# Four strips of 32 columns for each 64-row product, and P V in two bursts

## The chip, the cores and the metric

The kernel runs on one core of one Trainium2 chip. The metric is the time of one execution on the device, in microseconds (us). Times of this kernel are medians of a few executions; the profile is that of one execution, taken by the hardware profiler, and it has a time of its own.

The engines are named as the profile names them: PE (TensorE, matrix products), PEld (its weight loads, which overlap with the products), DVE (VectorE), ACT (ScalarE), POOL (GpSimd) and SP (SyncE, which here only issues DMAs and wake-ups). L709 is line 709 of the kernel.

## What is computed

A layer with two branches over a sequence of 2,048 tokens of 448 features. One branch is local attention with 16 heads of 28 features, in which each token sees itself and seven earlier ones, two apart; the other is a two-layer MLP with 1,792 hidden features. The branches are multiplied and added to the input.

```python
def _A_ref(x, wqkv, wo):                       # H = 16, Dh = 28, W, dil = 8, 2
    qkv = (x @ wqkv).reshape(B, S, 3, H, Dh).transpose(2, 0, 3, 1, 4)
    q, k, v = qkv[0], qkv[1], qkv[2]
    idx = pos[:, None] - (jnp.arange(W) * dil)[None, :]
    mask = idx >= 0
    ...
    logits = jnp.einsum("bhsd,bhswd->bhsw", q, kg) * Dh ** -0.5
    logits = jnp.where(mask[None, None, :, :], logits, -1e9)
    o = jnp.einsum("bhsw,bhswd->bhsd", _softmax(logits), vg)
    return o.transpose(0, 2, 1, 3).reshape(B, S, D) @ wo

def _B_ref(x, w1, b1, w2, b2):
    return gelu(x @ w1 + b1) @ w2 + b2

xn = _layernorm(A_x)
return A_x + _A_ref(xn, A_wqkv, A_wo) * _silu(_B_ref(xn, B_w1, B_b1, B_w2, B_b2))
```

Data and weights are bf16.

## The kernel before

**Tokens.** Even and odd tokens never see each other (the dilation is 2), so the sequence is split into two halves, and then into 16 tiles of 128 tokens and four chunks of 512. For the attention it is cut again into nine blocks (`VIS`), each with four windows of 57 (or 56) queries against 64 keys.

**The order is planned.** Nothing is issued where it is written. Each piece of work is a task with an engine (or several to choose from), an assumed cost in us, tasks it depends on, a priority, buffers it takes and gives back, and a function that issues the instructions. `_Plan.run` plays the tasks on a model of the engines: at each step it finds the task that could start first, looks at all that could start on that engine within 0.12 us of it, and picks the one with the highest priority. `emit` then issues all tasks in that order, so every engine runs a fixed program. The priorities are the tables `PRIO` and `LATER`. On PE, a task has a mode, the tiling shape in which PE's array is used. A task in another mode than the last is charged `SWITCH` = 0.095 us, one in the same mode gets `SAME` = 20 added to its priority.

**Dense products.** 448 features are three tiles of 128 rows and one of 64. The projections to q, k and v (L532 and L556) and the first MLP layer (L591) are computed as seven half products of 64 rows per output, not as three and a half whole ones. `pair` (L477) takes two outputs: four steps with the top rows of one beside the bottom rows of the other, then, after a wake-up sent through POOL or SP once the first four are done, three steps the other way round. In a step, two products of 64 rows by 128 columns run side by side, each into its own PSUM bank. The very first projections are made with 128 rows (`first_batch`). The second MLP layer (L627) and the output projection (L796) are 128-row products.

**Attention.** For each block, `scores_of` issues 64 products of 32 rows by 64 columns (L677) into four banks. ACT takes the exponential (L687), a 0/1 mask is multiplied in on DVE or POOL (L693), and `values_of` issues 64 products of 64 rows by 32 columns (L709), P V, into two banks. DVE then divides by the sums (L719 to L733). The keys' v rows are first moved to their places by DMAs that POOL issues (L354).

A PE task of the attention is a visit, made by `attn` (L743) from the list `VISITS` (L24): the scores of the first two blocks alone, and then P V of each block with the scores of the block two further on, in one task. A task with P V has mode 33, one with scores mode 32. It takes two banks for P V and four for scores, together, of eight.

**End.** `final_part` (L792) makes the output projection, multiplies, adds the input (DVE, or POOL for the first eight tiles) and writes out by SP.

Of the kernel before, what the change touches and what calls it, by code (L numbers as in the profile page):

```python
# [17 lines left out]
TILED = 30  # L18
SAME = 20
HOPS = ("POOL", ("SP", "POOL"))  # L20
MASK_ON = (("DVE", "POOL"), (0.4, 1.2))


def VISITS(bs):  # L24
    out = [[("S", b)] for b in bs[:2]]
    for i, b in enumerate(bs):
        out.append([("P", b)] + [("S", c) for c in bs[i + 2:i + 3]])
    return out
# [11 lines left out]
class _Task:  # L40
    __slots__ = ("eng", "cost", "deps", "fn", "prio", "take", "give", "slots",
                 "start", "end", "on", "ndep", "users", "tail", "seq", "table", "limit", "mode", "out")


class _Plan:
# [7 lines left out]
    def add(self, eng, cost, fn, deps=(), prio=0, take=(), give=(), tail=0.0, table=(), limit=None,  # L53
            mode=128):
# [5 lines left out]
        t.mode, t.out = mode, None  # L60
# [14 lines left out]
    def _at(self, t, e, free):  # L75
        at = free.get(e, 0.0)
        for p, n in t.take.items():
            if len(p.free) < n or p.fifo and p.fifo[0] is not t:
                return None
            at = max(at, sorted(p.free)[n - 1][0] + HOP)  # L80
        if t.table and self.table not in t.table:
            at += TABLE
        for d in t.deps:
            at = max(at, d.end - d.tail if d.on == e else d.end + HOP)
        if e == "PE" and t.mode != self.mode:
            at = max(at, free.get(e, 0.0) + SWITCH)
        return at

    def run(self):
# [6 lines left out]
        self.mode = 128  # L96
        ready = [t for t in self.tasks if not t.ndep]
        order = []
        while ready:
# [14 lines left out]
            tiled = first[2] == "PE" and self.mode < 64  # L114
            at, t, e, c = min(near, key=lambda k: (-k[1].prio - (TILED if tiled and k[1].mode < 64 else SAME if k[2] == "PE" and k[1].mode == self.mode else 0),
# [4 lines left out]
            if e == "PE" and t.fn is not None:  # L120
                self.mode = t.out or t.mode
# [43 lines left out]
def kernel(  # L165
# [80 lines left out]
    def ring(name, n, shape, dt=BF16, fifo=False):  # L246
# [24 lines left out]
        "project": (49.5, 205, 104, 52.5,),  # L271
        "project2": (147, 150, 101, 61,),
        "values": (89.5, 62.5, 21, 58,),
        "attn": (185, 179.5, 78, 174.5, 106.5, 106, 138.5, 136.5, 32.5,),
        "ff1": (185, 180, 84.5, 176.5, 66.5, 64.5, 156.5, 189.5, 203, 146, 76, 114.5, 77.5, 179.5,
            75.5, 118.5, 180.5, 14.5, 163, 68, 151, 115.5, 194.5, 167.5, 180, 188.5, 86, 93,),
        "gelu": (62.5, 22.5, 95, 92.5,),
        "ff2": (144, 162.5, 103.5, 142.5, 44.5, 112.5, 67, 5, 89, 106.5, 101.5, 75, 74, 55, 11.5,
            6.5,),
        "final": (140, 19.5, 70.5, 47, 112, 34.5, 23.5, 142.5, 73, 53, 198.5, 188.5, 81.5, 126.5,  # L280
            180, 71,),
        "norm": (37.5, 132, 179.5, 129.5, 74.5, 99, 161, 69, 63, 62, 43.5, 73, -5.5, 90, 133.5,
            150,),
        "loads": (166.5, 166, 188, 139.5, 54.5,),
        "stats": (47.5, -60, 180.5, 23, 127, 56, 188.5, 77, 197.5, -13.5, 185, 205.5, 138, 14, 52.5,
            138.5,),
        "turn_x": (108.5, -1, 28, 116, 210, 116.5, 131.5, 160, 41.5, 79.5, 70, 119, -4.5, 74.5,
            132.5, 111,),
        "turn_qk": (68.5, 112, 174.5, 90, 80, 6, 149.5, 60.5, 4, 140.5, 199.5, 96.5, 103, 166.5,
            140, 156,),  # L290
        "move_v": (81.5, 95, 23, 95, 18.5, 26.5, 8, 128, 29.5,),
        "copies": (50, 119.5, 58.5, 76, 32.5, 135.5, 43, 1, 87, 79.5, 129, 77, 32, 41.5, 135,),
    }
    LATER = {"swap": 135, "qk": 165, "v": 29.5, "gelu": 30.5, "exp": 55.5, "mask": -60, "pv": 45, "recip": -16.5, "os": 54.5, "y": 153.5, "tanh": 182.5, "g": 58, "sg": 183, "o": 120.5}
# [174 lines left out]

    def together(top, bottom):  # L470
        return [(f(), g()) for f, g in zip(top, bottom, strict=True)]
# [5 lines left out]
    def pair(a, b, prio, early=False):  # L477
# [11 lines left out]
        def f2(k):  # L489
            held["told"] = (nc.gpsimd if k.on == "POOL" else nc.sync).nop()  # L490
            for i in held["last"]:
                behind(held["told"], i)
        told = plan.add(HOPS[0] if early else HOPS[1], 0.06, f2, [t], 300)

        def f3(k):
            p, q = buf(p_b, t, 0), buf(p_b, t, 1)
            for i in together([part(b, q, kt, 0, kt + 4) for kt in range(3)], [part(a, p, kt, 1, kt + 4) for kt in range(3)])[0]:
                behind(i, held["told"])
# [5 lines left out]
    def first_batch(tiles, prio, tiles0=0):  # L504

        f = []
        for kt in range(3):
            for i, js in enumerate(tiles):
                def f1(k, kt=kt, i=i, js=js):
                    for q, j in enumerate(js):  # L510
                        j.part(buf(p_b, f[i] if kt else k, q), kt, 2, kt == 0, False)
# [14 lines left out]
    def qk_rows(t, which, prio):  # L526
        cs = slice(t * P, (t + 1) * P)

        def part(ps, kt, half, start, stop):
            r = half_rows(half)  # L530
            w = w_in[r, kt, which * D:(which + 1) * D] if kt < 3 else w_in3[r, 0, :]
            return nc.tensor.matmul(ps[:, :D], xnT[r, kt, cs], w, start=start, stop=stop)  # L532

        def evac(a, own, i):
# [6 lines left out]
            if len(t_row[t]) == 2:  # L541
                t_qk[t] = dma_T(qkT[:, :, :, cs].rearrange("p w g c -> p (w g) c"), lambda: b[:].rearrange("p w h c -> p (w h c)"),
                                t_row[t], PRIO["turn_qk"][t], None, 2, 1.9 if t < 3 else 3.8 if t == TPC else 2.0 if t == TPC + 1 else 1.27)
# [6 lines left out]
    def vproj(t, prio):  # L550
        k0 = t * P

        def part(ps, kt, half, start, stop):
            r = half_rows(half)
            w = w_in[r, kt, 2 * D:] if kt < 3 else w_in3[r, 1, :]
            return nc.tensor.matmul(ps[:, :D], xnT[r, kt, k0:k0 + P], w, start=start, stop=stop)  # L556
# [7 lines left out]
    def values(b):  # L564

        t_v[b], v_at[b] = [], []
        for i in range(2):
            first = None
            for w in range(2):
                k0 = VIS[b][2][w][i][1]  # L570
                for lo in sorted({k0, max(k0, (k0 + NK - 1) // P * P)}):
# [6 lines left out]
                    t_v[b].append(d)  # L578
# [6 lines left out]
    def ff1(c, mt, prio, gate):  # L585
# [3 lines left out]
        def part(ps, kt, half, start, stop):  # L589
            r = half_rows(half)  # L590
            return nc.tensor.matmul(ps[:], w1[r, kt, ms], xnT[r, kt, cs], start=start, stop=stop)  # L591
# [74 lines left out]
    def scores_of(b):  # L666
        q, nq, wins = VIS[b]

        def fn(banks):
            for i in range(2):  # L670
                for g in range(G):
                    for hl in range(4):
                        for w in range(2):
                            r = slice(32 * hl, 32 * hl + 32)
                            q0, k0 = wins[w][i]
                            c0 = (G * i + g) * nq
                            nc.tensor.matmul(banks[hl][NK * w:NK * w + NK, c0:c0 + nq], qkT[r, 1, g, k0:k0 + NK],  # L677
                                             qkT[r, 0, g, q0:q0 + nq], start=True, stop=True)
        return fn, [t_qk[t] for t in range(wins[0][0][1] // P, (q + 4 * nq - 1) // P + 1)]

    def weights_of(b, a, at, prio, gate):
# [3 lines left out]
        for hl in range(4):  # L685
            def f2(k, hl=hl):
                nc.scalar.activation(buf(p_E, k)[:, :n], buf(p_b, a, at + hl)[:, :n], ACT.Exp, scale=SCALE)  # L687
            e = plan.add("ACT", act(n), f2, [a] + gate, prio + LATER["exp"], take=(p_E,), give=((p_b, a, at + hl),), table=("exp",))
# [8 lines left out]
    def values_of(b, exps):  # L697
        nq = VIS[b][1]

        def fn(banks):  # L700
            for hl in range(4):
                E = buf(p_E, exps[hl])
                for i in range(2):
                    v = buf(*v_at[b][i])
                    for g in range(G):
                        for w in range(2):
                            r = slice(NK * w, NK * w + NK)
                            c0, c1 = (2 * hl + i) * nq, (G * i + g) * nq
                            nc.tensor.matmul(banks[w][32 * g:32 * g + 32, c0:c0 + nq], v[r, 4 * g + hl, :],  # L709
                                             E[r, c1:c1 + nq], start=True, stop=True)  # L710
        return fn, tuple((p_E, e, 0) for e in exps) + tuple(v_at[b])

    def output_of(b, po, i, w, prio):
# [4 lines left out]
        def f5(k):  # L718
            nc.vector.transpose(buf(p_dt, k)[:, :32 * m], buf(p_b, po, i)[:, :32 * m])  # L719
        d = plan.add("DVE", dve(32 * m), f5, [po], prio + LATER["recip"], take=(p_dt,))  # L720
# [11 lines left out]
        def f8(_):  # L732
            nc.vector.tensor_tensor(out=oT[:, :, q0:q0 + 2 * nq],  # L733
                                    in0=buf(p_b, po, i)[:, :n].rearrange("p (l q) -> p l q", l=4),
                                    in1=buf(p_dt, d)[:, :n].rearrange("p (l q) -> p l q", l=4), op=ALU.mult)
        o = plan.add("DVE", dve(n), f8, [rb], prio + LATER["os"], give=((p_b, po, i), (p_dt, d, 0)))
# [3 lines left out]
    last_visit = {"S": [], "P": []}  # L740
    state = {}

    def attn(b, what):  # L743

        deps, take, give, fns, cost = [], [], (), [], -SWITCH
        for n, (w, blk) in enumerate(what):
            if not n or what[n - 1][0] != w:
                cost += SWITCH
            cost += 0.215
            if not n:  # L750
                cost += 0.03
            at = len(take)
            if w == "S":
                fn, d = scores_of(blk)
                d = d + state["early"]
                take += [p_b] * 4
                fns.append(lambda k, fn=fn, at=at: fn([buf(p_b, k, at + i) for i in range(4)]))
            else:
                exps, masked = state[blk]
                fn, g = values_of(blk, exps)  # L760
                give += g
                d = masked + t_v[blk]
                take += [p_b] * 2
                fns.append(lambda k, fn=fn, at=at: fn([buf(p_b, k, at + i) for i in range(2)]))
            deps = deps + d + last_visit[w][-1:]

        def f1(k):
            for fn in fns:
                fn(k)
        prio = PRIO["attn"][b]  # L770
        a = plan.add("PE", cost, f1, deps, prio + (LATER["pv"] if what[0][0] == "P" else 0), take=take, give=give, tail=0.15,
# [195 lines left out]
```

## Time and profile before

| what | us |
|---|---|
| median of 3 executions (158.08 to 158.12) | 158.12 |
| the profiled execution | 157.98 |
| its span, from first to last instruction | 156.2 |
| PE busy in that span | 150.1 |
| lines 591 and 627 in the chain that ended last | 23% and 22% |
| lines 532, 556 and 796 in it | 11%, 6% and 7% |
| lines 677 and 709 (scores and P V) in it | 4% and 4% |

The chain that ended last is followed back from the last instruction, at each step to what released it, or to the instruction before it on its engine. Lengths of products on PE are modelled and overlap, so neighbouring lengths may add up to more than the time between their starts. A line `x64` in a timeline is 64 instructions merged into one row.

Of the 36 mask products (L693), 28 ran on POOL and 8 on DVE. The page's row of instruction packets (queue q8) gives number, MB and share of 16 engines' span: these bring the instructions of PE from memory.

### The profile page before, as it was taken

Reading aid. Unit: us, or ns where it says so; the run is one execution under the profiler, and the core shown is the slowest. Engines: PE = TensorE matmul, PEld = TensorE weight load, DVE = VectorE, ACT = ScalarE, POOL = GpSimd, SP = SyncE. Lnnn points to the kernel's source line nnn. Section 1 sums busy time; section 2 is a strip of 40 time slices with the busy share of each in tenths; the row PEclk is TensorE's granted clock in tenths of the full one; section 3 lists DMA queues with packets and bytes.
Section 4 is the critical chain, followed back from the end, with each engine's and each line's share of the span. In section 5 each row is a group of like instructions: output and inputs, shape, how many; then the busy total and the mean of one; then the engine's idle time right before and its main releaser. Section 6 shows DMA issues by size and latency. Waiting matters only on the chain.

```text
span 156.2 us, 5305 instructions
## 1 busy us (share of the span) xinstructions
PE 150.1 (96%) x2204; PEld 77.8 (50%) x2204; DVE 113.2 (72%) x259; ACT 83.3 (53%) x149; POOL 74.7 (48%) x123
## 2 busy tenths in 40 slices
PE   6999999999999999999999999999999999999980
PEld 2544454444455555455554644455556444545570
DVE  4789551486266758997799895109899996998992
ACT  3245867378889416444634149782496587051220
POOL 7854856000459408839261098389599780000000
PEclk9999999999999999999999999999999999999999
DMA  4999969999749443099039822123300100200211
GB/s 156 329 317 315 167 124 187 237 269 307 141 95 166 64 82 90 10 192 138 4 83 85 131 70 73 38 76 83 105 0 4 34 31 29 63 4 0 68 36 43
DMA packets 33575, 17.36 MB, mean 111 GB/s; under 512 B 25331, under 2 KB 32387, under 8 KB 33552
## 3 DMA queue, kind: packets, MB, share of 16 engines
q1 hardware_dynamic: 31472, 14.03, 41.3%
q0 software_dynamic: 1936, 2.88, 8.5%
q8 instruction: 17, 0.28, 0.8%
q10 hardware_dynamic: 144, 0.11, 0.2%
q14 instruction: 6, 0.05, 0.1%
HBM read 7.06 MB, written 1.84 MB: 57 GB/s over the span
## 4 chain that ended last, share of the span: by engine, by line
PE 80%; DVE 8%; DMA 3%; POOL 2%; issue 2%; ACT 1%; SPq 1%; DVEq 0%; ACTq 0%; POOLq 0%
PE bank L627 23%; PE bank L591 22%; PE bank L532 11%; PE bank L796 7%; PE bank L556 6%; PE bank L677 4%; PE bank L709 4%; PE bank L327 3%; DMA xnT<-xn 3%; POOL v L354 2%; DVE sg L801 2%; DVE o L807 1%; DVE w_in L659 1%; ACT E L687 1%; DVE xn L438 1%
## 5 line engine op out<-in xcount | busy, mean ns | idle before, releaser
L627 PE MATMUL bank<-w,h 128*128 128x448 bf16 (+1 forms) x238 | 45.2, 342 | 0.0
L591 PE MATMUL bank<-xnT,w 64*128 64x512 bf16 x392 | 44.7, 376 | 0.0
L595 ACT ACTIVATE h<-bank,b 128x512 bf16<-128x512 f32 x56 | 34.0, 689 | 12.9 <-PE bank L591 12.8
L354 POOL DMA_DIRECT2D v<-v_tok x52 | 27.6, 538 | 19.8 <-PE bank L709 9.0
L693 POOL TENSOR_TENSOR E<-E,m_gen 128x456 bf16<-128x456 bf16 x24 | 26.7, 1139 | 11.7 <-ACT E L687 9.5
L627 PEld LDWEIGHTS <-h 128*128 128x128 bf16 x238 | 22.3, 98 | 18.1 <-issue 0.4
L591 PEld LDWEIGHTS <-w 64*128 64x128 bf16 x392 | 19.1, 94 | 22.7 <-issue 1.1
L532 PE MATMUL bank<-w_in,xnT 64*128 64x448 bf16 (+1 forms) x212 | 24.3, 350 | 0.1
L687 ACT ACTIVATE E<-bank 128x456 bf16<-128x456 f32 (+1 forms) x36 | 17.0, 555 | 9.1 <-PE bank L677 9.1
L655 ACT ACTIVATE t<-y 128x448 f32<-128x448 f32 x15 | 8.7, 578 | 17.4 <-DVE y L649 17.4
L719 DVE STREAM_TRANSPOSE dt<-bank 128x480 f32<-128x480 f32 (+1 forms) x18 | 12.1, 671 | 5.6 <-PE bank L709 5.6
L532 PEld LDWEIGHTS <-xnT 64*128 64x128 bf16 (+1 forms) x212 | 10.6, 94 | 10.9 <-issue 1.1
L314 DVE CAST qk_tok<-bank 128x448 bf16<-128x448 f32 x16 | 9.4, 613 | 6.8 <-PE bank L532 6.8
L796 PE MATMUL bank<-wo,oT 128*128 128x448 bf16 (+1 forms) x68 | 14.1, 342 | 0.0
L312 ACT CAST qk_tok<-bank 128x448 bf16<-128x448 f32 x16 | 8.3, 533 | 10.6 <-PE bank L532 10.0
L556 PE MATMUL bank<-w_in,xnT 64*128 64x448 bf16 (+1 forms) x106 | 13.4, 349 | 0.0
L649 DVE TENSOR_TENSOR y<-bank,b 128x448 f32<-128x448 f32 x15 | 9.3, 620 | 4.9 <-PE bank L627 4.9
L728 DVE STREAM_TRANSPOSE dt<-rd 128x480 f32<-128x480 f32 (+1 forms) x18 | 12.1, 673 | 0.5
L733 DVE TENSOR_TENSOR oT<-bank,dt 128x456 bf16<-128x456 f32 (+1 forms) x18 | 11.3, 630 | 0.5
L404 DVE BATCH_NORM_STATS2 st<-x_sb 128x6 f32<-128x448 bf16 x16 | 9.6, 603 | 2.4 <-DMA x_sb<-in_A_x_dram 2.4
L438 DVE TENSOR_SCALAR xn<-x_sb,mv,rstd 128x448 bf16<-128x448 bf16 x16 | 6.3, 394 | 6.0 <-POOL rstd L426 5.8
L796 PEld LDWEIGHTS <-oT 128*128 128x128 bf16 x68 | 6.3, 98 | 6.3 <-issue 0.8
(62 smaller groups left out, 128.9 us busy)
## 6 DMA issues: line engine op xcount, KB each, us to landing
out_dram<-o SPq DMA_DIRECT2D x15, 112.0 KB, 1.7
w<-in_B_w_dram SPq DMA_DIRECT2D x2, 784.0 KB, 7.2
w<-in_B_w_dram SPq DMA_DIRECT2D x2, 672.0 KB, 7.0
x_sb<-in_A_x_dram SPq DMA_DIRECT2D x3, 448.0 KB, 6.3
v<-v_tok POOLq DMA_DIRECT2D x20, 64.0 KB, 2.5
w_in<-in_A_wqkv_dram SPq DMA_DIRECT2D x3, 336.0 KB, 4.3
w<-in_B_w_dram SPq DMA_DIRECT2D x4, 112.0 KB, 6.5
wo<-in_A_wo_dram POOLq DMA_DIRECT2D x4, 98.0 KB, 4.2
```

Of the source, the lines that this page charges most:

```text
L354: nc.gpsimd.dma_start(dst(k), src())
L532: return nc.tensor.matmul(ps[:, :D], xnT[r, kt, cs], w, start=start, stop=stop)
L556: return nc.tensor.matmul(ps[:, :D], xnT[r, kt, k0:k0 + P], w, start=start, stop=stop)
L591: return nc.tensor.matmul(ps[:], w1[r, kt, ms], xnT[r, kt, cs], start=start, stop=stop)
L595: nc.scalar.activation(buf(p_h, own, i)[:], buf(p_b, own, i)[:], ACT.Gelu_apprx_tanh, bias=b1[:, mt:mt + 1])
L627: nc.tensor.matmul(ps[:, :n], buf(*h_at[(c, mt)])[:, j * P:(j + 1) * P], w2[:, mt, cs], start=(mt == 0 and not biased), stop=(mt == NMT - 1))
L687: nc.scalar.activation(buf(p_E, k)[:, :n], buf(p_b, a, at + hl)[:, :n], ACT.Exp, scale=SCALE)
L693: (nc.gpsimd if k.on == "POOL" else nc.vector).tensor_tensor(out=E[:, :n], in0=E[:, :n], in1=m[:, :n], op=ALU.mult)
L719: nc.vector.transpose(buf(p_dt, k)[:, :32 * m], buf(p_b, po, i)[:, :32 * m])
L728: nc.vector.transpose(buf(p_dt, d)[:, :32 * m].rearrange("p (b c) -> p b c", c=32), buf(p_rd, r)[:, :m].unsqueeze(2).to_broadcast((P, m, 32)))
L733: nc.vector.tensor_tensor(out=oT[:, :, q0:q0 + 2 * nq], in0=buf(p_b, po, i)[:, :n].rearrange("p (l q) -> p l q", l=4), in1=buf(p_dt, d)[:, ...
L796: nc.tensor.matmul(ps[:, :n], oT[:, kt, t * P:(t + 1) * P], wo[:, kt, cs], start=(kt == 0), stop=(kt == KT - 1))
```

## The change

1. Each product of 64 rows and 128 columns is issued as four with 32 columns, into the four quarters of the bank's partitions, with the same moving operand (`strips`). `together` interleaves them: first strip of the one output, first strip of the other, second strip, and so on. Whole products of 128 rows stay as they are.
2. P V is issued in two tasks of 32 products, one for each `i` (half of the windows). They are in mode 64, the same as the dense half products. The first gives back one of the two v tiles, the second the other and the E tiles. It waits for all four masked E tiles and its own v tile only.
3. Scores are a task of their own with 64 products, in mode 32. Scores and P V bursts are marked `thin`; a thin task right after another is charged `APART` = 0.25 us. `VISITS` is gone: in each stage all scores are added, then all P V.
4. The masks are on DVE alone.
5. b2 is loaded as one row and spread over the partitions by POOL, where a DMA spread it.
6. All priorities are new, and some assumed costs of the transposing DMAs.

```diff
-TILED = 30
+APART = 0.25
-MASK_ON = (("DVE", "POOL"), (0.4, 1.2))
+MASK_ON = ("DVE", 0.4)
...
+        if e == "PE" and t.thin and self.thin:
+            at = max(at, free.get(e, 0.0) + APART)
...
+    def strips(out, lhsT, rhs, half, start, stop):
+        n = P if half > 1 else 32
+        return [lambda c=c: nc.tensor.matmul(out[c:c + n], lhsT[:, c:c + n], rhs, start=start, stop=stop) for c in range(0, P, n)]
+
     def together(top, bottom):
-        return [(f(), g()) for f, g in zip(top, bottom, strict=True)]
+        done = []
+        for f, g in zip(top, bottom, strict=True):
+            done.append([q() for pair in zip(f(), g(), strict=True) for q in pair])
+        return done
...
-            for i in held["last"]:
-                behind(held["told"], i)
+            behind(held["told"], held["last"][-1])
...
-            return nc.tensor.matmul(ps[:], w1[r, kt, ms], xnT[r, kt, cs], start=start, stop=stop)
+            return strips(ps[:], w1[r, kt, ms], xnT[r, kt, cs], half, start, stop)
...
-        def fn(banks):
+        def fn(banks, i):
+            v = buf(*v_at[b][i])
             for hl in range(4):
                 E = buf(p_E, exps[hl])
-                for i in range(2):
-                    v = buf(*v_at[b][i])
-                    for g in range(G):
-                        for w in range(2):
...
+                for g in range(G):
+                    for w in range(2):
...
+    def visit(what, fn, deps, prio, n, give):
+        parts = []
+        whole = what == "S"
+        for i in range(1 if whole else 2):
+            def f1(k, i=i):
+                own = (parts or [k])[0]
+                for q in range(2) if whole else (i,):
+                    fn([buf(p_b, own, j) for j in range(n)], q)
+            parts.append(plan.add("PE", 0.5 if whole else 0.15, f1, deps[i] + deps[1] * whole + [(parts or [last_visit[what]])[-1]], prio + i * LATER["half"],
+                                  take=() if i else (p_b,) * n, give=give[i] + give[1] * whole, tail=0.15, mode=32 if whole else 64, thin=True))
+        last_visit[what] = parts[-1]
+        return parts[0], parts[-1]
...
-    t_b2 = dma("POOL", b2[:], B_b2.rearrange("(o d) -> o d", o=1).to_broadcast((P, D)), 112, 82, turned)
+    b2r = p_o.bufs[-1]
+    t_b2r = dma("POOL", b2r[:1], B_b2.rearrange("(o d) -> o d", o=1), 1, 82, turned[:1])
+    t_b2 = plan.add("POOL", 0.5, lambda _: nc.gpsimd.partition_broadcast(b2[:], b2r[:1], channels=P), [t_b2r], 82)
```

## The prediction

> **What bounds the kernel.** I read the page first: busy shares, slices, chain of waits.
>
> ```profile
> span 156.2 us, 5305 instructions
> PE 150.1 (96%) x2204; PEld 77.8 (50%) x2204; DVE 113.2 (72%) x259; ACT 83.3 (53%) x149; POOL 74.7 (48%) x123
> PE   6999999999999999999999999999999999999980
> PEclk9999999999999999999999999999999999999999
> PE 80%; DVE 8%; DMA 3%; POOL 2%; issue 2%; ACT 1%; SPq 1%; DVEq 0%; ACTq 0%; POOLq 0%
> q8 instruction: 17, 0.28, 0.8%
> ```
>
> TensorE (PE) is busy in every slice but the ends, at full clock, and has 80% of the chain. So the time is the sum of what PE issues, plus some 4.5 us after its last product (151.7 to 156.2). A change counts by what it takes off PE's row; anything on another engine counts only where PE comes to wait for it.
>
> Next the timeline of PE alone (start, length, line, shape, count). Lengths overlap, so I use distances between starts.
>
> ```profile
> 57.62 0.68 PE L709 MATMUL bank<-E,v 64*32 64x57 bf16 x64
> 58.23 0.76 PE L677 MATMUL bank<-qkT 32*64 32x57 bf16 x64
> 58.92 2.82 PE L627 MATMUL bank<-w,h 128*128 128x448 bf16 x14
> ...
> 76.80 2.82 PE L532 MATMUL bank<-w_in,xnT 64*128 64x448 bf16 x28
> 79.46 2.81 PE L556 MATMUL bank<-w_in,xnT 64*128 64x448 bf16 x28
> 82.11 2.81 PE L532 MATMUL bank<-w_in,xnT 64*128 64x448 bf16 x28
> 84.85 1.69 PE L796 MATMUL bank<-wo,oT 128*128 128x448 bf16 x8
> ```
>
> Read three prices. A step of two 64-row products side by side: (79.46-76.80)/14 = 0.190 us at 448 columns; the group from 13.24 to 16.27 gives 3.03/14 = 0.216 us at 512. A change of tiling shape: 84.85-82.11 = 2.74 against 14 x 0.190 = 2.66, so about 0.09 us, paid by whoever comes next. P V: 58.23-57.62 = 0.61 us for 64 tiny products.
>
> Then stretches of that P V visit, each counted from its start, in the windows of line 709 (length; PE busy, products started so far; clock; DMA):
>
> ```profile
> 57.62:57.74 0.12, 0.12 (x32) 1.00 0.18 22
> 57.62:57.84 0.22, 0.22 (x32) 1.00 0.11 12
> 57.62:58.11 0.49, 0.49 (x64) 1.00 0.05 5
> ```
>
> This is the centre of the case. The first 32 products start within 0.12 us (3.7 ns each); then nothing starts for 0.10 us; the other 32 need 0.27 us (8.3 ns each), and the drain into the next shape fills the 0.61. So 32 products lie ready when a visit begins, and whatever is beyond must be fed at 8.3 ns.
>
> **Part 1, P V in two bursts of 32.** Before: five visits alone at 0.61 (3.05), two double visits of 1.29 and 1.25 us, together 5.59; seven entries from another shape at 0.09 make 6.2 us. After, 18 bursts. One between strips of its own shape costs 0.12 us, no drain on either side, and the stretch without starts lies under the next dense step of 0.19. One put among 128-row products costs 0.09 + 0.12 + about 0.12 (the step from a visit's last product to the next shape: 0.61-0.49) = 0.33. Ends: all in 64-row stretches, 18 x 0.12 = 2.2; none, 5.9. The planner charges 0.095 for a switch and adds 20 to the rank of work in the standing mode, so I take two thirds inside: 12 x 0.12 + 6 x 0.33 = 3.4. **Gain 2.8 us**, ends 0.3 and 4.0.
>
> **Part 2, scores apart.** The nine visits take 0.64, 0.63, 0.69, 0.75, 0.63, 0.71, 0.63, 1.20 and 0.63, in all 6.5 us. Five come straight after a P V visit, so their entry is in its 0.61, and three of these are slowed; the 1.20 holds a wait of some 0.57 for an exponential (ACT). After: 9 x 0.635 = 5.7, and 5 x 0.09 for entries now paid. **Gain 0.35 us**; from -0.2, if such a wait returns, to 0.8. A P V task no longer takes six of eight banks at once, but two, which makes its waiting less likely.
>
> **Part 3, strips.** 392 + 200 + 100 = 692 products of 64 rows become 2,768, so 2,076 more products and as many weight loads, in 346 steps of eight. Does a step stay 0.190 or 0.216? It is set by streaming if eight strips run together. Nearest row: the first 32 of P V. Eight strips of 57 columns per 8 x 3.7 = 30 ns; one alone streams 57 of 448 columns, 57/448 x 190 = 24 ns. So nearly all eight run at once in exactly this shape, weight loads included (33 of them in the same 0.12 us). Even when fed at the slow 8.3 ns, a step needs 66 ns, a third of what it streams. So the strips cost nothing while streaming; what hides them is the 0.19 us of columns. They cannot gain: streaming stays. At the end of each 64-row stretch the eighth strip ends 8 x 3.7 = 30 ns late: some ten stretches, **0.3 us lost**. Upper end: rival B.
>
> More instructions have to be brought in. The page gives 17 packets for 4,408 PE instructions (259 each), in 0.8% of 16 x 156.2 us, thus 1.2 us a packet. Strips use 16 instructions a step, 259 in 3.1 us. It fits 2.6 times over, and the double P V visit at 104.63 ran 256 in 1.29 us without a gap of a microsecond. I count 0, at most 1.
>
> The Trainium skill's page "TensorEngine Tiling (Array Packing)", section "Restrictions", speaks against this part: column tiling turns off fast weight load. Its page "TensorE: Matmul & The Clock Gate", section "LDWEIGHTS", gives columns/1.2 in ns, thus 27 ns for 32 columns. Were the eight loads of a step to go one by one, they would need 213 ns where 448 columns stream in 190, and 150 such steps would lose 3.5 us: by that rule most of the gain is gone. The windows show 33 loads started in 0.12 us, so loads of different tiles do not queue like that, and I go by the trace.
>
> **Part 4, masks.** 28 mask products (the 24 of this row, and four with m_mid, 4.1 us) leave GpSimd (POOL) for VectorE (DVE). The rows of lines, then two of the windows of DVE from 60 to 150 us:
>
> ```profile
> L693 POOL TENSOR_TENSOR E<-E,m_gen 128x456 bf16<-128x456 bf16 x24 | 26.7, 1139 | 11.7 <-ACT E L687 9.5 <-PE bank L532 1.3 <-PE bank L591 0.8
> L693 DVE TENSOR_TENSOR E<-E,m_gen 128x456 bf16<-128x456 bf16 x4 | 1.5, 388 | 0.0
> L659 DVE SCALAR_TENSOR_TENSOR w_in<-t,y 128x448 bf16<-128x448 f32 x7 | 6.7, 960 | 0.4 <-ACT t L655 0.3
> ...
> 120.00:130.00 10.00, 9.72 (x17) 1.00 0.08 25
> ...
> sum 90.00, DVE 73.52; mean DVE 8.17
> ```
>
> On DVE: 28 x 0.39 = 10.9 us more. Relief: the seven L659 products at 960 ns ran mostly while POOL multiplied masks (113 to 128 us), others of this size take some 0.62, so 7 x 0.34 = 2.4 back. From 60 to 150 us DVE then has 73.5 + 10.9 - 2.4 = 82 of 90 us, or of 87 once PE is shorter. It fits with 5 us to spare, and four masks take 1.5 instead of 4.1 us, so P V is ready earlier. The cover is thin from 110 to 130, where DVE has 8.99 and 9.72 of 10 us: twelve of the masks lie there, so 18.7 + 12 x 0.39 - 2.4 = 21.0 of 20 us, and 23.4 without the relief. What is late there next is the release of PSUM banks, and PE waits behind it, in order. I charge **0.5 us**, half of the 1.0, since the order moves and DVE was 5.2 us idle before 105; ends 0 and 3.4. POOL, relieved of 30.8 us, sends the v moves and the wake-ups between halves no later than now.
>
> **Part 5, b2 and the order.** b2 arrives as one row and is spread by POOL. Before, its DMA was issued at 24.8 us and first used at 49.05. The broadcast has no row; POOL operations range from 0.1 to 1.6 us; what queues behind it are v moves. Even ten times the dearest fits in the 24 us, so 0. SP's queue is not touched by it. The new ranks move everything; what they bring in waits or alternations of 64- and 128-row stretches (42 changes of shape now) I can't read from the profile: 0, with ±1.5 us in the range.
>
> One wait is narrower: the first burst of a block needs all four masked E tiles and its first v tile, the second burst only the other v tile. Behind a late mask stands all of PE, since it issues in order; that is the 0.5 above.
>
> **Sum.** -2.8 - 0.35 + 0.3 + 0.5 = -2.35 us. Span 156.2 becomes 153.85. The profiled execution took 157.98, 1.78 beyond its span, and the median is 0.14 above it: 153.85 + 1.78 + 0.14 = **155.8 us**, 1.5% less. A measurement here can tell about 0.2%, or 0.32 us.
>
> **Rivals.**
> A, more than forecast: nearly every burst in strips (4.0) and no stall in exchange (0.8), nothing lost on DVE: -4.5, **153.6 us**. For it: 40% of dense PE time after 46 us is 64-row. Against: around 46 to 60 us only 128-row products lie between the visits.
> B, slower: **the strips' step grows**, in all 346 steps of lines 591, 532 and 556, because eight moving operands are read at once for long. The burst shows eight together only for 57 columns. It decides from 2.35/346 = 7 ns a step on. The burst's round of eight took 30 ns where streaming needs 24: were these 6 ns a price per round, a step would lose 6 ns, or 2.1 us in all; were they a price per column, 6 x 448/57 = 47 ns, or 16 us. Between ends so far apart I take the geometric middle, 17 ns: 5.9 us, **161.7 us**. Against it: the first eight products started within 0.03 us, and a gap between starts in one step is covered by the columns of the one before.
> C, no measurable change: bursts land mostly in 128-row stretches (0.3) and VectorE's load eats the rest: **158.0 us**.
>
> **How the numbers follow.** Forecast 0.54, with its own range 154.6 to 157.3; A 0.18; B 0.18; C 0.10. Faster by over 0.2% (below 157.8): forecast, A and a little of C, 0.74. Within: 0.06. Slower: B and the rest of C, 0.20. The range runs from 152.8 (A with the free 1.5 of the order halved) to 159.6 (C, and B up to 11 ns a step), which leaves out the dearer half of B and the ends.
>
> **What would show it.** Right: the distance between starts of eight-strip steps stays 0.190 and 0.216; 32 of P V start within 0.12 us and a dense product within 0.02 after; line 709 occurs in 18 pieces; fewer than 42 changes of shape; DVE near 120 us. Wrong: steps of 0.2 and more (B); DVE at 10 of 10 us over a long stretch with PE waiting for banks (C); gaps of 1 us in PE with an instruction packet in flight.

## The result, and the profile after

The changed kernel takes **188.65 us** (187.35 to 191.58, 4 runs) where the kernel before takes 158.1: a ratio of 1.191, 95% interval 1.185 to 1.198. Medians here and below are of all runs; ratios and intervals leave out runs more than 1.5% above the quickest of their kernel (here the one of 191.58, at a lower clock). The forecast was 155.8 with a range of 152.8 to 159.6. It is wrong by more than its sign: the loss is 31 us.

The page of the profile after, the rows that answer to those shown of before:

```profile
span 185.3 us, 9455 instructions
PE 157.9 (85%) x4282; PEld 88.4 (48%) x4282; DVE 115.4 (62%) x278; ACT 86.4 (47%) x157; POOL 45.3 (24%) x97
PE   7998797348971999898788999999699999979991
PEclk9999999995798599999999999999999999999999
PE 79%; issue 12%; DMA 4%; SPq 2%; DVE 1%; POOL 0%; POOLq 0%; DVEq 0%
q8 instruction: 33, 0.54, 1.2%
```

PE is no longer always busy: slices show 1, 3 and 4 tenths, the clock falls to half in places (5, 7, 8 and 5 tenths as slice means), and 12% of the chain is "issue", time in which PE waits for nothing that the profile shows. The packets of instructions have gone from 17 to 33, and PE's products and weight loads from 4,408 to 8,564: one packet for some 260 of them, as before.

Where PE stands still is seen in its timeline (start, length, line, shape, count, and in brackets the idle time before):

```profile
12.09 4.28 PE L466 MATMUL bank<-xnT,w 64*32 64x512 bf16 x145
17.23 0.84 PE L466 MATMUL bank<-xnT,w 64*32 64x512 bf16 x23 [0.86 <-issue]
...
31.22 1.86 PE L466 MATMUL bank<-w_in,xnT 64*32 64x448 bf16 x65
35.98 3.22 PE L466 MATMUL bank<-w_in,xnT 64*32 64x448 bf16 x128 [2.90 <-issue]
42.45 2.81 PE L466 MATMUL bank<-w_in,xnT 64*32 64x448 bf16 x55 [3.25 <-issue]
44.69 9.88 PE L466 MATMUL bank<-xnT,w 64*32 64x512 bf16 x288
59.69 7.26 PE L466 MATMUL bank<-xnT,w 64*32 64x512 bf16 x160 [5.12 <-POOLq L491]
```

Between two stops lie exactly 128 strips (35.98 to 42.45), 256 instructions with their weight loads. And a stretch of the same timeline in which nothing is late:

```profile
121.62 6.27 PE L466 MATMUL bank<-xnT,w 64*32 64x512 bf16 x224
127.67 0.45 PE L706 MATMUL bank<-E,v 64*32 64x56 bf16 x32
127.95 1.09 PE L466 MATMUL bank<-xnT,w 64*32 64x512 bf16 x32
128.82 0.45 PE L706 MATMUL bank<-E,v 64*32 64x56 bf16 x32
```

224 strips are 28 steps: (127.67-121.62)/28 = 0.216 us, the step of whole products. **The strips stream at full speed; what fails is their supply.**

I numbered all that the trace has of PE's queue in the order of starts: products, weight loads and the 26 waits on semaphores and drains among them. A stop gets the number of the instruction just ahead of the product that ends it. Of the 16 places where PE goes over 0.43 us from one product to the next after its first strip, 15 have the number 193 or 194 modulo 256: they lie 256 instructions, or a multiple of 256, apart. I call the 256 instructions that one packet brings a page. Beside each such stop stands one instruction packet. Some of them (us; the last two columns are the distance from the end of the stop before to the packet's start, and from its landing to the next product):

| number | last product | packet | next product | stop to packet | landing to product |
|---|---|---|---|---|---|
| 450 | 15.99 | 14.43 to 15.72 | 17.23 | | 1.5 |
| 706 | 20.18 | 19.34 to 20.30 | 21.51 | 2.1 | 1.2 |
| 1474 | 32.74 | 33.39 to 34.43 | 35.98 | 3.6 | 1.6 |
| 1730 | 38.85 | 40.05 to 41.15 | 42.45 | 4.1 | 1.3 |
| 4033 | 88.66 | 87.77 to 88.88 | 90.38 | | 1.5 |
| 4289 | 93.25 | 91.61 to 92.91 | 94.39 | 1.2 | 1.5 |
| 6594 | 133.14 | 132.15 to 133.13 | 134.50 | 1.3 | 1.4 |

One packet is on its way at a time. Moving it takes 0.9 to 1.4 us, but a full turn also has the way to the packet's start (1.1 to 1.5 us, up to 4.1 while the DMA engines are full before 45 us) and from its landing to the next product (1.2 to 1.6): 3.5 to 4 us in quiet, 3.7 to 6.5 in the crowd. 256 instructions of strips last 16 steps, 3.0 to 3.5 us. So in a long stretch of strips PE catches up with its supply at every page; where other work lies between, it does not stop (15 stops for 33 packets).

**The ledger.** The 15 gaps are 21.8 us from product to product, some 2.2 of which is ordinary step: 19.6 lost. The sixteenth gap, 5.5 us at 54.2, ends with a wake-up on POOL: 5.3 lost. Behind the longest gaps the clock is halved, as two windows show (length; PE, PEld, DVE, ACT and POOL busy; clock; DMA):

```profile
41.40:48.20 6.80, 5.75 (x120) 2.96 (x128) 2.78 (x9) 1.50 (x3) 0.00 (x0) 0.50 0.38 81
58.50:65.30 6.80, 5.61 (x112) 2.30 (x120) 2.10 (x9) 2.34 (x4) 2.78 (x4) 0.50 0.22 43
```

Half of 5.75 and of 5.61 is 5.7 lost. Together 30.6; the span grew by 185.3-156.2 = 29.1. By this sum all the rest of the change is worth about -1.5 us. The terms are not quite independent: at half clock a page lasts longer (42.45 to 48.36, 5.9 us), and its packet comes in time (e9 below stops at the end of this page and of the next two, 2.1 us, where the changed kernel does not). e8 measures the rest by itself.

### The profile page after: what moved, and what is told of

Its sections match the earlier page's. It is cut to its first block, busy times and chain, and to the rows that moved or that the text cites. A ratio compares the mean times of both kernels' runs of the same rounds, so it can differ in the third digit from the quotient of the medians.

```text
span 185.3 us, 9455 instructions
## 1 busy us (share of the span) xinstructions
PE 157.9 (85%) x4282; PEld 88.4 (48%) x4282; DVE 115.4 (62%) x278; ACT 86.4 (47%) x157; POOL 45.3 (24%) x97
## 4 chain that ended last, share of the span: by engine, by line
PE 79%; issue 12%; DMA 4%; SPq 2%; DVE 1%; POOL 0%; POOLq 0%; DVEq 0%
PE bank L466 43%; PE bank L626 24%; PE bank L773 7%; DMA w<-in_B_w_dram 4%; PE bank L675 3%; PE bank L706 3%; SPq L341 2%; DVE sg L778 0%; DVE o L784 0%; DVE g L658 0%; POOL sd L419 0%; PE bank L624 0%; POOLq L491 0%; DVEq L778 0%
## 5 line engine op out<-in xcount | busy, mean ns | idle before, releaser
L466 PE MATMUL bank<-xnT,w 64*32 64x512 bf16 x1568 | 52.4, 404 | 8.6 <-POOLq L491 5.1
L466 PE MATMUL bank<-w_in,xnT 64*32 64x448 bf16 (+1 forms) x1218 | 38.8, 360 | 10.4 <-issue 10.4
L594 ACT ACTIVATE h<-bank,b 128x512 bf16<-128x512 f32 x56 | 34.6, 687 | 27.4 <-PE bank L466 27.2
L466 PEld LDWEIGHTS <-w 64*32 64x32 bf16 x1568 | 25.1, 98 | 31.1 <-issue 11.9
L626 PEld LDWEIGHTS <-h 128*128 128x128 bf16 x238 | 22.3, 98 | 19.2 <-issue 1.2
L466 PEld LDWEIGHTS <-xnT 64*32 64x32 bf16 (+1 forms) x1218 | 20.2, 94 | 22.3 <-issue 14.1
L306 ACT CAST qk_tok<-bank 128x448 bf16<-128x448 f32 x22 | 11.1, 534 | 21.1 <-PE bank L466 15.2
L308 DVE CAST qk_tok<-bank 128x448 bf16<-128x448 f32 x10 | 6.1, 623 | 19.6 <-PE bank L466 16.5
L706 PE MATMUL bank<-E,v 64*32 64x57 bf16 (+1 forms) x576 | 8.3, 188 | 3.2 <-issue 3.2
L706 PEld LDWEIGHTS <-v 64*32 64x32 bf16 x576 | 7.1, 91 | 7.0 <-issue 5.1
L691 DVE TENSOR_TENSOR E<-E,m_gen 128x456 bf16<-128x456 bf16 x28 | 9.8, 390 | 0.1
```

What stands on the lines that cost most here:

```text
L306: nc.scalar.copy(o, i)
L466: return [lambda c=c: nc.tensor.matmul(out[c:c + n], lhsT[:, c:c + n], rhs, start=start, stop=stop) for c in range(0, P, n)]
L594: nc.scalar.activation(buf(p_h, own, i)[:], buf(p_b, own, i)[:], ACT.Gelu_apprx_tanh, bias=b1[:, mt:mt + 1])
L626: nc.tensor.matmul(ps[:, :n], buf(*h_at[(c, mt)])[:, j * P:(j + 1) * P], w2[:, mt, cs], start=(mt == 0 and not biased), stop=(mt == NMT - 1))
L691: (nc.gpsimd if k.on == "POOL" else nc.vector).tensor_tensor(out=E[:, :n], in0=E[:, :n], in1=m[:, :n], op=ALU.mult)
```

## The experiments

All are timed against the kernel before on the same chip (medians 158.1 us). Theory F: the supply of instructions. Theory B: the broadcast of b2 on POOL.

**e1, whole products in the changed kernel.**

```diff
-        n = P if half > 1 else 32
+        n = P
```

> The changed kernel in the same order on every engine, but with each 64-row product issued whole (4,410 PE instructions instead of 8,562). Theory F (feed): the packets that bring 256 PE instructions arrive too slowly for strips; in the profile after, 15 gaps of 0.6 to 3.6 us stand at instruction numbers 193 or 194 modulo 256, worth 19.7 us, and one half-clock stretch behind them 2.9 us. Then this kernel takes 188.65 - 19.7 - 2.9 = 166 us, +1 to 2 for drains around P V: 164 to 169, with no gap at 194 modulo 256 left and the one wait for a wake-up on POOL still there. Theory B (the loss is the broadcast of b2 and what it delays): it stays above 182. Theory O (the new order is at fault): above 180 as well, with gaps elsewhere.

168.88 us, 1.069 (1.065 to 1.074). F holds: no gap at a fixed number is left. What it has over 166 is not so much the 1 to 2 us added for drains as the other wait, which grew from 5.5 to 10.5 us from product to product; on PE and on POOL:

```profile
37.70 3.28 PE L466 MATMUL bank<-xnT,w 64*128 64x512 bf16 x28
51.06 5.29 PE L466 MATMUL bank<-xnT,w 64*128 64x512 bf16 x32 [10.08 <-POOLq L491]
```

```profile
40.31 0.52 POOL L873 PARTITION_BROADCAST b<-o  x1 [12.46 <-PE bank L466]
40.68 2.85 POOL L348 DMA_DIRECT2D v<-v_tok  x5
50.65 0.30 POOL L419 TENSOR_SCALAR sd<-mv,eps_t 128x4 f32<-128x4 f32 x1 [7.12 <-issue]
```

The broadcast itself takes 0.52 us. But the next ordinary operation of POOL (L419) starts 7.1 us after the last DMA issue, behind an instruction of the trace named MODIFY_POOL_CONFIG at 43.6, which the kernel before has only at its start. The wake-up for PE (L491) is queued behind L419 and goes out at 50.99. The changed kernel shows the same: MODIFY_POOL_CONFIG at 52.1, L419 at 59.28, PE goes on at 59.69.

**e4, strips in the kernel before, and e6, no strips but as many instructions.** e4 puts `strips` into the kernel before and nothing else. e6 cuts the same products along the moving columns, so the tiling shape stays 64x128:

```diff
-        n = P if half > 1 else 32
-        return [lambda c=c: nc.tensor.matmul(out[c:c + n], lhsT[:, c:c + n], rhs, ...) for c in range(0, P, n)]
+        w = out.shape[-1]
+        n = w if half > 1 else w // 4
+        return [lambda c=c: nc.tensor.matmul(out[:, c:c + n], lhsT, rhs[:, c:c + n], start=start and not c, stop=stop and c + n == w) for c in range(0, w, n)]
```

> The kernel before, same order and tasks, with strips as the only edit. Theory F: the same stalls as in the changed kernel, at 193 or 194 modulo 256, some 15 to 23 us: 174 to 182 us, steps between stalls at 0.190 and 0.216. Theory S (strips stream more slowly, rival B of the prediction): steps over 0.2 at 448 columns and no gaps at fixed instruction numbers. Theory O: 158 to 160, the strips being harmless.

> The kernel before with each 64-row product cut in four along the moving columns (112 or 128 each), in the old shape of 64 rows by 128 columns: as many instructions as with strips, no column tiling, the same columns streamed. Theory F: the stalls of the strips come back without strips, at 193 or 194 modulo 256, 174 to 185 us (up to 2.5 us more for 346 steps with three more starts of 2.5 ns each). Theory S (column tiling is the cause): 158 to 161 us and no such gaps.

e4: 182.6 us, 1.151 (1.144 to 1.158); a little over what was expected. Its profile, of the run that took 186.19 where the others took 180.89 to 182.79, has 15 gaps at 193 or 194 modulo 256, 22.3 us. e6: 180.39 us, 1.141 (1.135 to 1.146), with ten gaps at 193 to 195 modulo 256, 15.8 us. Its timeline of PE:

```profile
30.20 5.37 PE L473 MATMUL bank<-w_in,xnT 64*128 64x112 bf16 x211
38.63 0.83 PE L473 MATMUL bank<-w_in,xnT 64*128 64x112 bf16 x13 [3.06 <-issue]
39.17 4.71 PE L473 MATMUL bank<-xnT,w 64*128 64x128 bf16 x115
44.28 0.90 PE L473 MATMUL bank<-xnT,w 64*128 64x128 bf16 x26 [0.40 <-issue]
```

13 + 115 = 128 products between two stops again, in the old shape. So neither column tiling nor the new order is the cause; the number of instructions is. Halved clock behind the long gaps is part of both losses: e6 has three stretches of 3.4 us at half clock, at most 5.1 us lost. I did not split the rest of e6's.

**e10, the supply by itself.** 1,024 tiny products of P V's shape are added at the end of the kernel before (they use a spare tile as both operands and write to banks that are done).

```diff
+        for i in range(1024):
+            w, g = i % 2, i // 2 % 4
+            r = slice(64 * w, 64 * w + 64)
+            nc.tensor.matmul(p_b.bufs[w][32 * g:32 * g + 32, :57], src[r, 32 * g:32 * g + 32], src[r, :57], start=True, stop=True)
```

> The kernel before, unchanged, with 1,024 further products of P V's shape (64 rows by 32 columns, 57 moving columns, 2,048 PE instructions, 8 packets) at its end, where the DMA engines carry only the last outputs; their results go to two banks that nothing reads any more. PE was done at 151.7 us. If the only limit on many small instructions is what the second half of a P V visit showed, 8.3 ns a product, they take 8.5 us: PE ends near 160 and the run takes about 162 us. Theory F: from page to page it takes 3.5 to 4 us in quiet (in the changed kernel, 1.2 from the stop's end to the next packet's start, 1.0 to 1.3 to move it, 1.2 to 1.5 to the next product), so 1.1 us of work and a gap of 2.4 to 2.9 us at every 256 instructions: 8 x 3.7 = 30 us less what lies ready, PE ends at 175 to 182 us.

182.95 us (one run), span 181.1, PE ends at 179.8: as theory F had it. In its timeline of PE:

```profile
153.43 1.66 PE L941 MATMUL bank<-h 64*32 64x57 bf16 x183 [0.92 <-DVE sg L801]
157.45 1.21 PE L941 MATMUL bank<-h 64*32 64x57 bf16 x128 [2.35 <-issue]
161.18 1.27 PE L941 MATMUL bank<-h 64*32 64x57 bf16 x128 [2.52 <-issue]
164.63 1.27 PE L941 MATMUL bank<-h 64*32 64x57 bf16 x128 [2.19 <-issue]
...
179.00 0.80 PE L941 MATMUL bank<-h 64*32 64x57 bf16 x72 [2.46 <-issue]
```

The purest picture of it: 128 products start within 1.0 us, then a stop; from start to start 3.73, 3.45, 3.73, 3.45, 3.46 and 3.73 us. From 159.62 on the clock is half, and the turns stay as they were, so it is not PE's own speed that sets them. With the DMA engines nearly free (2% busy), 256 of these instructions in a long run cost 3.45 to 3.73 us, 14 ns each. The first piece has 183 products because the run crosses its first page boundary without a stop: one page lies ready. That reserve is what a lone burst lives on.

**e7, two strips of 64 columns in the kernel before** (64 for 32 in `strips`).

> The kernel before with two strips of 64 columns for each 64-row product: 8 instructions a step, so 256 last 6.1 to 6.9 us. Theory F: a packet came every 3.4 to 3.7 us at the least where PE waited for it late in the run, and up to 6.6 us early, where the DMA engines are full: nearly all is covered, 158 to 162 us, with gaps at 193 or 194 modulo 256 only before 50 us if at all. A cost per added product, or per added instruction, would give a third of what four strips lost (692 added where there were 2,076): 158.1 + 24.5/3 = 166 us.

163.38 us, 1.035 (1.031 to 1.039): above what F expected, below the third. Two gaps at 193 or 194 modulo 256 are left, at 109 and 140 us, 1.9 us together. Most of the rest of the 5.3 us is waits on other things: transposed xn (1.4 us), w_in (0.8), a wake-up on SP (0.9). So a page of 6 to 7 us is covered nearly everywhere; why loads landed later here stays open.

**e2 and e9, the broadcast replaced.** e2 puts back the DMA that spreads b2, and the planner makes another order. e9 keeps every task of the changed kernel and issues the DMA in the broadcast's place:

```diff
-    ... lambda _: nc.gpsimd.partition_broadcast(b2[:], b2r[:1], channels=P), [t_b2r], 82)
+    ... lambda _: nc.gpsimd.dma_start(b2[:], B_b2.rearrange("(o d) -> o d", o=1).to_broadcast((P, D))), [t_b2r], 82)
```

> The changed kernel with b2 spread by a DMA as before (replanned, since POOL's tasks differ). Theory B: the broadcast makes POOL load its code twice (5.6 and 7.1 us), the second load holds up a wake-up for 5.3 us of PE time and the idle PE then runs at half clock for 6.8 us, worth 2.8: 188.65 - 8.1 = 180.5, 178 to 183, with the gaps at 194 modulo 256 still there. If the broadcast is harmless: 187 to 190.

> The changed kernel, strips and all, in its own order, with the DMA in the place of the broadcast (e2 also changed the plan). Theory B: the wait of 5.5 us at 54.2 and the 2.8 us of half clock behind it go: 180.5, 178.5 to 183.5. If feeding alone sets the time there and the wait was covered: 186 to 189.

e2: 186.04 us, 1.167 (1.159 to 1.174), a miss: the wait for the wake-up is gone and twelve gaps at 193 or 194 modulo 256 stay (16.6 us), but the other order has new gaps, the largest 1.7 and 2.3 us near 147 us, where PE waits for oT from DVE and drops to half clock. It says little, since it changes two things. e9: 178.88 us (178.85, 178.90 and 180.21, and 174.06 for the profiled run; no ratio was taken): the median is within what was expected, the profiled run below it. In its profile no gap over 0.43 us but those at 193 or 194 modulo 256 (17, together 20.1 us) and no half clock before the outputs at the end are left. The expectation left the first half-clock stretch of the changed kernel standing; in this run that one is missing too, though PE stood for 2.98 us at the same page. The other three runs have no profile, so what they have beyond it stays open.

**e5, the broadcast in the kernel before.**

> The kernel before with the one-row load and the broadcast of b2 as the only edit (replanned). Theory B: POOL changes its code twice; the second change, ahead of the rstd of chunk 2, holds the wake-ups behind it for some 7 us while PE has little else: 3 to 10 us of PE wait and half clock behind it, 162 to 171 us. If the broadcast's place among POOL's work matters more than the change of code itself, and it falls in a stretch without wake-ups: 158 to 159.

167.42 us, 1.057 (1.054 to 1.061). One wait of PE for the wake-up on POOL (L490) of 7.3 us, from 43.4 to 50.7, and half clock behind it (47.7 to 54.5). The broadcast alone, with the planner's order around it, loses 9.3 us.

**e8, bursts, masks and order without strips and broadcast** (both edits above, in the changed kernel).

> The changed kernel with whole products (as in e1) and, in the place of the broadcast instruction on POOL, a DMA that spreads b2; the order of PE, DVE, ACT and SP is that of e1. Theory B (broadcast): e1's one big wait of PE, 10.46 us at 40.6 for a wake-up on POOL, goes, and so does the half clock after it (44.2 to 54.5, of which PE ran in the last 3.4 us, so 1.7 us lost): 168.88 - 10.3 - 1.7 = 156.9, 155.5 to 159. That would be what bursts, masks and order are worth without strips and broadcast. If the wait has another cause (rstd late by itself, v moves): 165 to 169.

**156.99 us, 0.992 (0.990 to 0.995)**: faster than both kernels, and close to the ledger's number (-1.1 us where it had -1.5). PE has no gap over 0.53 us. Against e1, from which it differs in nothing but the broadcast instruction, it gains 168.88-156.99 = 11.9 us: so much did the broadcast cost there. Its timeline of PE shows what a burst costs among whole products:

```profile
64.01 0.34 PE L706 MATMUL bank<-E,v 64*32 64x57 bf16 x32
64.28 0.74 PE L466 MATMUL bank<-w_in,xnT 64*128 64x448 bf16 x6
64.95 0.31 PE L706 MATMUL bank<-E,v 64*32 64x57 bf16 x32
65.20 6.98 PE L466 MATMUL bank<-w_in,xnT 64*128 64x448 bf16 x72
```

0.25 to 0.27 us from burst to dense product, and 0.09 for the entry.

**e11, strips only between two bursts.** e8, with strips in the nine dense groups that stand between two bursts, so that the shape does not change there.

```diff
+            t.between = 0 < n < len(pe) - 1 and all(q.thin and q.mode == 64 for q in (pe[n - 1], pe[n + 1]))
...
+            cut["n"] = 32 if k.between else P
```

> e8 (whole products, DMA in the broadcast's place), with strips only in a dense group that stands between the two bursts of one or two P V tasks: 54 products in nine groups, 324 more PE instructions. Theory F: so few that no packet is late. Each such group saves two changes of shape, 0.18 us, nine times 1.6; a burst behind strips took 0.28 where one among whole products takes 0.245, so 0.3 back: 157.0 - 1.3 = 155.7, 155.0 to 156.6. If strips cost anything by themselves, 157 or more.

157.05 us, 0.994 (0.991 to 0.996): no gain, a miss. No packet was late. The timeline, at the same place as e8's above:

```profile
63.62 0.34 PE L713 MATMUL bank<-E,v 64*32 64x57 bf16 x32
63.84 0.79 PE L471 MATMUL bank<-w_in,xnT 64*32 64x448 bf16 x24
64.41 0.47 PE L713 MATMUL bank<-E,v 64*32 64x57 bf16 x32
64.81 6.98 PE L471 MATMUL bank<-w_in,xnT 64*128 64x448 bf16 x72
```

From the first burst to the product after the second: 64.81-63.62 = 1.19 us; in e8 65.20-64.01 = 1.19. What the drains save (0.57 for 0.67 in the dense group, 0.22 for 0.27 from the first burst to it), the second burst loses (0.40 for 0.25). Windows of that burst, counted from its start:

```profile
64.40:64.52 0.12, 0.11 (x22) 1.00 0.00 0
64.40:64.64 0.24, 0.23 (x29) 1.00 0.00 0
64.40:64.80 0.40, 0.39 (x32) 1.00 0.00 0
```

Behind whole products 32 started within 0.12 us in the kernel before (57.62) and within 0.13 at 64.95 in e8; behind strips 22 do.

**e12, all masks on DVE in the kernel before** (`MASK_ON = ("DVE", 0.4)`).

> The kernel before with all masks on DVE as the only edit (replanned). The prediction charged 0.5 us, ends 0 and 3.4; the changed kernel's traces show no wait of PE for DVE and lines 658 at 0.62 us instead of 0.96. Neutral: 157.3 to 158.9. If the old order needs POOL's help: 159 to 162.

159.07 us, 1.007 (1.004 to 1.009): slower by 1.0 us in that order, a little outside what was expected. PE waits 0.7 us for oT from DVE there.

## Why the prediction was wrong, point by point

**The step that failed** is the second paragraph of Part 3: "1.2 us a packet. Strips use 16 instructions a step, 259 in 3.1 us. It fits 2.6 times over, and the double P V visit at 104.63 ran 256 in 1.29 us without a gap of a microsecond. I count 0, at most 1." The arithmetic is right, and both uses of the rows are wrong. A packet's time in the DMA row is the time that it moves; its turn, from one stop's end to the next, is 3.45 to 3.73 us in quiet (e10) and 3.7 to 6.5 in the changed kernel before 45 us, because the next packet starts only 1.0 to 1.5 us after PE has gone on (up to 4.1 before 45 us) and PE goes on only 1.2 to 1.6 us after it has landed. And a visit of 256 instructions shows what the page lying ready allows, once; it is no rate. Measured in place of 0: 19.6 us, and 2.9 more by the clock (the ledger); e9 against e8, where only strips differ, gives 178.88-156.99 = 21.9 us (17.1 with e9's quickest run); e4 and e6 show it without the rest of the change, and e6 without strips. The rival that should have stood there was named only as a sign to look for ("gaps of 1 us in PE with an instruction packet in flight").

The Trainium skill's page "Runtime: NRT & Kernel Launch", section "Instruction fetch mechanics", says that instructions are refilled in blocks of 256, the next one fetched while the current is executed, and calls the cost mostly hidden. The first two agree with every row above; "hidden" does not hold at 16 instructions in 0.19 to 0.22 us, and the measurement decides. I did not weigh that page, though it bears on a change that adds 4,152 instructions.

**Part 5** failed too: "Even ten times the dearest fits in the 24 us, so 0." I asked when b2 is needed. The cost is not in b2 but in POOL's change of code and back, and in who is queued behind the second: Part 4's "the wake-ups between halves no later than now" is refuted by L491 in e1. Measured: 5.3 us and 2.8 by the clock in the changed kernel, 9.3 in e5, 11.9 between e1 and e8. The Trainium skill's "GPSIMD Engine Reference", section "2.1 Instruction dispatch", gives about 6 us for newly loaded code of this engine; on the way back to ordinary operations e1 shows 7.1 between DMA issue and L419, the changed kernel 7.2 and e5 7.4, and the measurement decides.

**Streaming, and rival B's mechanism**: right to dismiss. Steps are 0.216 after, as computed from the timeline above; eight strips with eight weight loads cost what two products cost. The rule on fast weight load that was weighed there would have made the 448-column step longer; (64.41-63.84)/3 = 0.19 us in e11 shows that it is not. (The 3.5 us counted from that rule would have taken all of the 2.35 us forecast, not most of it.) The 0.3 us for the ends of the stretches no run separates. That B's number, 161.7, is on the right side is no merit: its cause is not the one at work.

**Part 1**, 2.8 us: mis-sized. A burst among whole products was put at 0.33 and is 0.25 + 0.09 = 0.34. A burst among strips was put at 0.12 and is 0.28 (127.95-127.67) where no packet is late, since fewer than 32 products lie ready; the stretch without starts is not hidden. The two thirds were about right: 13 of the changed kernel's 18 bursts have strips on both sides. With 12 x 0.28 + 6 x 0.34 = 5.4 instead of 3.4, the gain is 0.8. In e8, with all 18 among whole products, 18 x 0.34 = 6.1 against 6.2, a gain of 0.1 where the low end had 0.3.

**Part 2**, 0.35 us: nine visits of 0.63 to 0.64 us in e8, and the wait of 0.57 did not return. Right.

**Part 4**, 0.5 us: neutral in the changed orders (PE's only wait for DVE in e8 is the 1.2 us at the start that the kernel before has too), 1.0 in the old one (e12). The relief is right, and larger than counted: the L659 products at 960 ns are now L658 at 620 and less. DVE's busy time rose by 2.2 us (115.4) where 8.5 were counted, but the new order also gave casts of 4.4 us to ACT; in e12, with one cast fewer on DVE, it rose by 5.2 (118.4).

**The new order**: counted 0, with ±1.5. e8's gain of 1.1 us is bursts, scores, masks and order together; I did not separate them, since another order comes with each.

## What to carry to other kernels

Count PE's instructions, not only its columns: a long stretch that uses 256 of them in less than about 4 us (products and weight loads counted) ran here at the rate of its supply, and while the DMA engines were full, a page needed up to 6.7 us (e4, 36.8 to 43.5 us). A short burst lives on what lies ready, so its speed is no proof for a stretch. And before an operation is given to an engine that also passes wake-ups, look for what it does to the next operation there, not at its own 0.5 us.

## What the runs showed of the hardware

Supply stops are exact: the same residue modulo 256, within one or two, in seven kernels with different orders (the changed one, e2, e4, e6, e7, e9, e10). A packet's landing is followed by the next product 1.2 to 1.7 us later in all of them, crowded or not; what grows in the crowd is the time before its start, from 1.0 to 4.3 us.

Every stop in which PE stood for more than 3 us was paid twice: 3.06 and 3.25 us in e6, 3.12 in e4, 3.25 and 5.12 in the changed kernel, 7.29 in e5 and 10.08 in e1 each had half clock that began during it or within 1 us of its end and lasted 3.4 us (e4, e6), 6.8 (changed kernel, e5) or 10.2 (e1). Below 3 us it went either way: half clock after 2.80 and 1.88 us in e4, none after 2.98 in e9 and 2.90 in the changed kernel. What decides there the runs do not show.

Sharing a tiling shape between dense work and small bursts saved 0.15 us on a pair of bursts (e11) and gave it back, since behind strips fewer small products start at once (22 to 24 of 32).
